# K and V tiles with 32 adjacent keys per partition in a decode attention backward kernel

## The chip, the cores and the metric

The kernel runs on one core of a Trainium2 chip. The metric is the device time of one execution in microseconds; the figure for the kernel before is the median of three runs. A profile of one further execution comes with it: every instruction with its engine, its time and what it waited for, and the packets of the sixteen DMA engines. Engines are PE (TensorE, with PEld for its weight loads), DVE (VectorE), ACT (ScalarE), POOL (GpSimd) and SP (SyncE, which here only issues transfers). HBM is the chip's main memory; SBUF, with 128 partitions, and PSUM, into which PE writes, are the memories on the core.

## The reference

One decode step (four sequences, one new token each, width 512) through a layer norm, an attention over a cache and a gated feed-forward, summed, and then the gradients of all inputs:

```python
def _fwd_reference(A_x, A_k_cache, A_v_cache, A_wq, A_wo, B_x, B_w_gate, B_w_up, B_w_down):
    def _A_ref(x, k_cache, v_cache, wq, wo):
        B, Sq, D = x.shape
        Hq, Dh = 32, 128
        Hkv, Sk = k_cache.shape[1], k_cache.shape[2]
        W = min(4096, max(256, Sk // 4))
        rep = Hq // Hkv
        q = (lambda x, *d: x.transpose(*d))((x @ wq).reshape(B, Sq, Hq, Dh), 0, 2, 1, 3)
        k = jnp.repeat(k_cache[:, :, Sk - W:, :], rep, axis=1)
        v = jnp.repeat(v_cache[:, :, Sk - W:, :], rep, axis=1)
        scores = jnp.einsum("bhqd,bhkd->bhqk", q, k) * (Dh ** -0.5)
        p = _softmax(scores, axis=-1)
        o = jnp.einsum("bhqk,bhkd->bhqd", p, v)
        return (lambda x, *d: x.transpose(*d))(o, 0, 2, 1, 3).reshape(B, Sq, Hq * Dh) @ wo

    def _B_ref(x, w_gate, w_up, w_down):
        return (_gelu(x @ w_gate) * (x @ w_up)) @ w_down

    x = A_x
    xn = _layernorm(x, axis=-1)
    return x + _A_ref(xn, A_k_cache, A_v_cache, A_wq, A_wo) + _B_ref(xn, B_w_gate, B_w_up, B_w_down)
...
    _out, _vjp = jax.vjp(_f, A_x, A_k_cache, A_v_cache, A_wq, A_wo, B_w_gate, B_w_up, B_w_down)
    _grads = _vjp(grad_out)
```

Caches are 4 x 8 x 4096 x 128 in bf16: four sequences (called batches), eight kv heads, 4096 keys of 128 numbers. Only the last W = 1024 keys take part, so the gradients of the two caches are zero in their first 3072 keys and have to be written there all the same. There are 32 query heads, four to a kv head.

## The kernel before

**Stages.** First the feed-forward, forward and backward, with its three weights and their gradients; then attention, batch by batch; then an end with the output, the gradient of x and the gradients of wo and wq. Only the transfers on SP are in an order written out by hand; on the other engines a scheduler orders the instructions by their place in the program and by when it thinks they are ready, and each engine then runs its own list in that order.

**Tiles of K and V.** load_kv brings one batch's K or V (2.1 MB) as a tile of 128 partitions x 8 heads x J = 8 keys x 128 numbers. Key m*8 + j lies in partition m, so each row of a transfer is 8 keys, 2 KB. Two transfers, of four heads each, make a tile (L233). K has two buffers, ka and kb, V one, va. The first K comes by SP's queue, all other tiles by POOL's.

**Attention of one batch.** scores(0, b) makes q times k, scores(1, b) makes dy times v: four VectorE transposes a call (t32, L93), each turning 1024 32-bit words a partition in blocks of 32 x 32 into a scratch tile (two buffers), and 16 matmuls against a block-diagonal tile bd after each; head pair c goes to the partitions of quarter c. softmax makes the probabilities P_b (bf16) and P_f. turned brings P_b's keys onto the partitions by 32 small matmuls and one copy from PSUM through evac. odq multiplies this with V (k = 0, giving the attention output) or K (k = 1, giving the gradient of q), 32 matmuls with the results of head pair c in quarter c; the masks om and oms then pick the right head of a pair. spread makes four scaled copies of P_b, and dvdk from these the gradients of V and K: 64 matmuls, 16 copies out of PSUM into two staging tiles (stg, four buffers for the whole kernel) and two stores of 1 MB on POOL, in rows of 2 KB (L106). softmax_d makes dS_b, which goes through turned, odq and spread in the same way for K.

**Order around the loads.** va for batch b+1 is requested once odq(0, b) has read va; K for batch b+2 once odq(1, b) has read its buffer. zeros puts stores of the zero part on SP's queue (32 in all, 1.5 MB each, rows of 12 KB), no more than three under way, and most of them wait for the landing of the load that is named with them, so that a load goes ahead of them:

```python
                pT = turned(P_b, 0)
                o_done = odq(0, b, pT)
                if b + 1 < B:
                    zeros((2, 2, 4)[b], load_kv(b + 1, 1, att, "va", nc.gpsimd, single_packet=True))
```

**The planner.** evac sends a copy out of PSUM to ScalarE or VectorE, whichever has the smaller sum of charges so far (load["act"], load["dve"]); transposes and other large steps add their own charges.

**bd and dyBD.** bd has two buffers for q (k = 0) and two for dy (k = 1); POOL clears them once at the start of attention and refill writes the blocks. dyBD, 2048 bf16 a partition, is the block-diagonal dy for the products with w_down and wo; it is last read by the do matmuls, before the first batch.

Of the kernel before, what the change touches and what calls it, by code (L numbers as in the profile page):

```python
# [9 lines left out]
ALU = mybir.AluOpType  # L10
# [8 lines left out]
def kernel(  # L19
# [140 lines left out]
    def mask(name, n, in_):  # L160
# [9 lines left out]
    hm = mask("hm", Q, ident_f[:].rearrange("p (h d) -> p h d", d=4))  # L170
    omt = const.tile([P, NQ, 2], FP32, name="omt")
    TT(out=omt[:], in0=gmask[:].rearrange("p (c g) -> p c g", g=2), in1=bm[:].unsqueeze(2).broadcast_to([P, NQ, 2]),
       op=ALU.mult)
    om = mask("om", 2, omt[:].rearrange("p c g -> p g c"))
    oms = const.tile([P, 2], FP32, name="oms")
    TS(out=oms[:], in0=om[:], scalar1=scale, scalar2=None, op0=ALU.mult)
    gmask_b = const.tile([P, G], BF16, name="gmask_b")
# [34 lines left out]
    t32(dyP, pairs(dy_b[:]), 256)  # L212
    dyBD = const.tile([P, NPB, 2, P], BF16, name="dyBD")
    nc.gpsimd.memset(dyBD[:], 0.0)
    dyPb = dyP.bitcast(BF16).rearrange("p n (x r) -> p n r x", r=2)
# [11 lines left out]
    def load_kv(b, k, pool, tag, eng, **kw):  # L227
        d_, src = ((k_t, A_k_cache), (v_t, A_v_cache))[k]
        tl = pool.tile([P, G, J, Dh], BF16, name=tag, tag=tag)
        for hf in range(2):  # L230
            hs = slice(hf * G // 2, (hf + 1) * G // 2)
            with tc.high_priority():
                d = eng.dma_start(out=tl[:, hs].rearrange("p g j d -> p g (j d)"),  # L233
                                  in_=src[b, hs, K0:Sk, :].rearrange("g (m j) d -> m g (j d)", j=J), **kw)
        d_[b] = tl
        return d
# [148 lines left out]
    with tc.tile_pool(name="mid", bufs=1, reuse_waits="tile") as mid:  # L385
# [4 lines left out]
        with tc.tile_pool(name="att", bufs=1, reuse_waits="tile") as att:  # L390
# [7 lines left out]
            for k in range(2):  # L398
                bd.append([])
                for u in range(2):  # L400
                    t_ = att.tile([P, DPB, NQ, 2, 2, Q], BF16, name=f"bd{k}{u}")
                    nc.gpsimd.memset(t_[:], 0.0)
                    bd[k].append(t_)
            selh = att.tile([P, P + 4], FP32, name="selh")
# [61 lines left out]
            def get_d(ps, u):  # L466
                l_ = dsc[:, 512:640] if u == 0 else dsc[:, 640:768]
                mm(ps[:].rearrange("p b d -> p (b d)"), l_, dM.rearrange("p b e k -> p (b e k)"))

            spread_rows(1, get_d)  # L470

# [9 lines left out]
            def scores(k, b):  # L481
# [4 lines left out]
                for g2 in range(2):  # L486
                    for e in range(2):
                        sc = scratch()
                        t32(sc[:].rearrange("p (c j m) -> p c j m", c=NQ, j=J), src[:, g2:G:2, :, e * Q:(e + 1) * Q], 1024)
                        sb = sc[:].bitcast(BF16).rearrange("p (c n r) -> p c r n", c=NQ, r=2)  # L490
                        for r in range(2):
                            for c, q in enumerate(quad):
                                mm(ps[q, :], t_[:, e, c, g2, r, :], sb[:, c, r, :], g2 == 0 and e == 0 and r == 0,
                                   g2 == 1 and e == 1 and r == 1, (0, Q * c))
                return ps[:]

            def spread(src, k):
# [3 lines left out]
                for a in range(4):  # L501
                    TS(out=sp[:, :, a, :], in0=src[:].rearrange("p (j m) -> p j m", j=J), scalar1=amask[:, a:a + 1],  # L502
                       scalar2=None, op0=ALU.mult)
                return sp

            def turned(src, k):

                ps = bank("pT_ps", "x", (P, J, Q))
                for j in range(J):
                    for a, q in enumerate(quad):  # L510
                        mm(ps[q, j, :], src[:, j * Q:(j + 1) * Q], selp[:, a].rearrange("p c r -> p (c r)"), pos=(0, Q * a))
                pT = att.tile([P, J, Q], BF16, name="pT", tag=f"pT{k}")
                evac(pT[:], ps[:], NJ)
                return pT
# [4 lines left out]
            def softmax(S):  # L519
# [18 lines left out]
                nc.vector.reciprocal(out=rr[:], in_=es_ps[:])  # L538
                P_b = att.tile([P, NJ], BF16, name="P_b", tag="P_b")
                nc.scalar.activation(out=P_b[:], in_=E_f[:], func=ACT.Copy, scale=rr[:, 0:1])  # L540
                P_f = att.tile([P, NJ], FP32, name="P_f", tag="P_f")
                p_done = nc.scalar.activation(out=P_f[:], in_=E_f[:], func=ACT.Copy, scale=rr[:, 0:1])
                load["act"] += 1400
                return P_f, P_b, p_done

            def softmax_d(P_f, dP):
# [7 lines left out]
                nc.vector.tensor_copy(out=cc[:], in_=gs_ps[:])  # L554
                dS_b = att.tile([P, NJ], BF16, name="dS_b", tag="dS_b")
                STT(out=dS_b[:], in0=dP, scalar=cc[:, 0:1], in1=P_f[:], op0=ALU.subtract, op1=ALU.mult)
                load["dve"] += 1200
                return dS_b
# [18 lines left out]
            def odq(k, b, pT):  # L577
# [3 lines left out]
                for j in range(J):  # L581
                    for c, q in enumerate(quad):
                        mm(ps[q].rearrange("p g d -> p (g d)"), pT[:, j, :], src[:, 2 * c:2 * c + 2, j, :],
                           j == 0, j == J - 1, (0, Q * c))
                mk = (om, oms)[k]
                t_ = att.tile([P, Dh], FP32, name="odt", tag=f"odt{k}")
# [189 lines left out]
```

## Time and profile before

| what | value |
|---|---|
| median of three runs | 283.15 us (282.53 to 283.21) |
| the profiled execution | 283.66 us, span 281.3 us |
| busy: PE, DVE, ACT, POOL | 184.8, 162.6, 124.3, 60.2 us |
| moved by DMA | 112.21 MB, mean 399 GB/s |
| HBM read, written | 30.93 MB, 81.01 MB |
| DMA issues: zeros; dv, dk, dwo, dwq; va; kb; ka | 32 of 1536 KB; 24 of 1024 KB; 8; 4; 4 of 1024 KB |
| from issue to landing, median: zeros, va, kb | 13.8, 15.8, 20.6 us |

The span runs from the first instruction to the last of the profiled execution. A row of digits divides it into 40 equal slices, each digit the busy share in tenths (9 is 90% or more). q1 is the queue of transfers issued by SP, q0 that of POOL; the last figure of a queue is the time that its packets took, as a share of sixteen engines' span. Matmuls overlap, so that PE's busy time is not a measure of a full PE. In a line of a group, "out<-in" names the tiles, then come partitions x elements, the count, and after the bar the busy time in all (us), the mean of one (ns), and the idle time of the engine before them with what ended it.

### The profile page before, as it was taken

How to read it: one execution, taken by the hardware profiler on the slowest of the kernel's cores; microseconds unless marked ns; L12 is line 12 of the kernel's file. 1: busy time of each engine (PE TensorE's matmuls, PEld its weight loads, DVE VectorE, ACT ScalarE, POOL GpSimd, SP SyncE). 2: the span in 40 equal slices, each digit the busy share in tenths (PEclk: the TensorE clock that was granted, in tenths of full speed). 3: DMA queues.
4: the chain of work that ended last, by engine and by line, in shares of the span. 5: the costliest groups of instructions: out<-in, count | busy, mean ns of one | idle time of the engine just before them, and what ended most of it. 6: DMA issues, size and time to landing. Idle time of an engine off the chain costs nothing.

```text
span 281.3 us, 4405 instructions
## 1 busy us (share of the span) xinstructions
PE 184.8 (66%) x1733; PEld 75.0 (27%) x1733; DVE 162.6 (58%) x309; ACT 124.3 (44%) x245; POOL 60.2 (21%) x135
## 2 busy tenths in 40 slices
PE   0327899869354999559946642953357997944980
PEld 0102363233122624224311321321034232410210
DVE  1869748899796616445028350574396104495980
ACT  1133855720102489525724402722341768544880
POOL 8500110088182213130040060020020020200210
PEclk9999965558855557555555555555555557775555
DMA  7999999999999999999999999999989999999996
GB/s 251 422 445 438 396 392 416 431 425 414 389 430 424 426 364 400 314 379 416 421 406 395 428 429 412 351 430 429 424 354 423 420 404 398 401 412 404 410 384 250
DMA packets 17027, 112.21 MB, mean 399 GB/s; under 512 B 1384, under 2 KB 1648, under 8 KB 11376
## 3 DMA queue, kind: packets, MB, share of 16 engines
q1 hardware_dynamic: 6688, 66.46, 56.9%
q0 software_dynamic: 10176, 45.35, 41.2%
q8 instruction: 13, 0.21, 0.3%
q10 hardware_dynamic: 144, 0.13, 0.1%
q14 instruction: 6, 0.05, 0.1%
HBM read 30.93 MB, written 81.01 MB: 398 GB/s over the span
## 4 chain that ended last, share of the span: by engine, by line
DMA 32%; issue 14%; DVE 10%; PE 9%; ACT 4%; POOL 2%; POOLq 0%; ACTq 0%; DVEq 0%
DMA out_dram<-stg 19%; DMA va<-in_A_v_cache_dram 11%; DVE scr L93 6%; ACT stg L88 3%; PE dwq_ps L117 2%; DMA out_dram<-ztile 2%; PE od_ps L117 2%; PE sc_ps L117 1%; DVE stg L89 1%; POOL out_dram L106 1%; PE kv_ps L117 1%; DVE dqs L603 1%; PE dwo_ps L117 1%; PE es_ps L117 1%; DVE spr L502 1%
## 5 line engine op out<-in xcount | busy, mean ns | idle before, releaser
L88 ACT CAST stg<-kv_ps 128x512 bf16<-128x512 f32 x118 | 63.8, 602 | 57.5 <-DMA out_dram<-stg 29.6
L106 POOL DMA_DIRECT2D out_dram<-stg x30 | 19.7, 659 | 146.2 <-ACT stg L88 105.0
L117 PE MATMUL sc_ps<-scr,bd 128*32 128x256 bf16 x256 | 24.2, 396 | 21.8 <-DVE scr L93 21.8
L117 PE MATMUL kv_ps<-dm,spr 32*128 32x256 bf16 x128 | 28.5, 399 | 6.8 <-ACT stg L88 5.0
L117 PE MATMUL kv_ps<-qm,spr 32*128 32x256 bf16 x128 | 24.5, 371 | 12.1 <-ACT stg L88 11.6
L93 DVE STREAM_TRANSPOSE scr<-va 128x1024 uint32<-128x1024 uint32 x16 | 18.8, 1216 | 12.6 <-DMA va<-in_A_v_cache_dram 12.5
L117 PEld LDWEIGHTS <-spr 32*128 32x128 bf16 x256 | 12.1, 101 | 46.8 <-issue 42.4
L117 PEld LDWEIGHTS <-bd 128*32 128x32 bf16 x256 | 8.1, 107 | 34.7 <-issue 34.1
L88 ACT CAST stg<-dwg_ps 128x448 bf16<-128x448 f32 x26 | 12.5, 554 | 5.8 <-PE dwg_ps L117 3.4
L88 ACT CAST stg<-dwo_ps 128x512 bf16<-128x512 f32 x18 | 10.0, 588 | 11.2 <-PE dwo_ps L117 8.9
L117 PE MATMUL dwo_ps<-dy_b,oSP 32*128 32x512 bf16 x32 | 9.4, 522 | 7.8 <-ACT stg L88 6.6
L89 DVE CAST stg<-kv_ps 128x512 bf16<-128x512 f32 x10 | 6.6, 678 | 12.0 <-DMA out_dram<-stg 6.0
L93 DVE STREAM_TRANSPOSE scr<-ka 128x1024 uint32<-128x1024 uint32 x8 | 9.6, 1228 | 6.1 <-DMA ka<-in_A_k_cache_dram 3.9
L233 POOL DMA_DIRECT2D va<-in_A_v_cache_dram x8 | 6.0, 756 | 31.6 <-PE od_ps L117 27.7
L93 DVE STREAM_TRANSPOSE scr<-kb 128x1024 uint32<-128x1024 uint32 x8 | 9.8, 1231 | 5.1 <-DMA kb<-in_A_k_cache_dram 4.5
L117 PE MATMUL do_ps<-scr,dyBD 128*128 128x512 bf16 x32 | 10.2, 460 | 2.1 <-DVE scr L93 2.0
L117 PE MATMUL dwq_ps<-dqSP,xn_b 32*128 32x512 bf16 x32 | 10.7, 586 | 0.9
L588 DVE SCALAR_TENSOR_TENSOR odt<-od_ps,oms,odt 128x128 f32<-128x128 f32 x4 | 1.4, 340 | 17.2 <-ACT odt L587 17.0
L89 DVE CAST stg<-dwo_ps 128x512 bf16<-128x512 f32 x14 | 9.2, 680 | 3.5 <-issue 2.3
L89 DVE CAST stg<-dwq_ps 128x512 bf16<-128x512 f32 x15 | 9.9, 689 | 1.7 <-PE dwq_ps L117 1.4
L117 PEld LDWEIGHTS <-pT 128*32 128x32 bf16 x256 | 9.2, 140 | 5.2 <-ACT pT L88 2.3
L88 ACT CAST stg<-dwq_ps 128x512 bf16<-128x512 f32 x17 | 9.8, 585 | 1.3 <-PE dwq_ps L117 0.6
(196 smaller groups left out, 317.1 us busy)
## 6 DMA issues: line engine op xcount, KB each, us to landing
out_dram<-ztile SPq DMA_DIRECT2D x32, 1536.0 KB, 13.8
out_dram<-stg POOLq DMA_DIRECT2D x24, 1024.0 KB, 12.8
va<-in_A_v_cache_dram POOLq DMA_DIRECT2D x8, 1024.0 KB, 15.8
out_dram<-stg POOLq DMA_DIRECT2D x6, 896.0 KB, 10.9
wq_sb<-in_A_wq_dram SPq DMA_DIRECT2D x1, 4096.0 KB, 24.1
wo_sb<-in_A_wo_dram SPq DMA_DIRECT2D x1, 4096.0 KB, 34.7
kb<-in_A_k_cache_dram POOLq DMA_DIRECT2D x4, 1024.0 KB, 20.6
ka<-in_A_k_cache_dram SPq DMA_DIRECT2D x2, 1024.0 KB, 43.4
```

What stands on the lines that cost most here:

```text
L88: return nc.scalar.copy(out=out, in_=in_)
L89: return nc.vector.tensor_copy(out=out, in_=in_)
L93: nc.vector.transpose(out=out, in_=in_)
L106: d = eng.dma_start(out=out, in_=in_, **kw)
L117: nc.tensor.matmul(out, lhsT=lhsT, rhs=rhs, start=first, stop=last, **kw)
L233: d = eng.dma_start(out=tl[:, hs].rearrange("p g j d -> p g (j d)"), in_=src[b, hs, K0:Sk, :].rearrange("g (m j) d -> m g (j d)", j=J), **kw)
L502: TS(out=sp[:, :, a, :], in0=src[:].rearrange("p (j m) -> p j m", j=J), scalar1=amask[:, a:a + 1], scalar2=None, op0=ALU.mult)
L588: done = STT(out=t_[:], in0=ps[:, 1, :], scalar=mk[:, 1:2], in1=t_[:], op0=ALU.mult, op1=ALU.add)
L603: nc.vector.tensor_copy(out=dqs[q, :, :, :, a * B + b], in_=d3v[q])
```

## The change

K and V tiles become 128 partitions x 2 heads x 32 keys x 128 numbers: partition 4m + c holds keys 32m to 32m + 31 of the two heads of pair c. A row of a transfer is 32 adjacent keys, 8 KB; a tile takes four transfers of 32 partitions each, one for each c, onto every fourth partition.

What follows from the layout: the transposes in scores write in the order (j, m, c) into a tile that is laid out c, j, m; the scores' columns are then ordered key-in-row j (32) by row m (8 of each quarter). turned makes P transposed four times as large (it needs the probabilities of each key on the partitions of all four c, of which a mask, pmask, keeps one): P_b and dS_b are written four times over (1024 instead of 256 elements), 128 matmuls replace 32, and two masked multiplies on VectorE replace one copy by the planner. odq keeps its count of matmuls; a quarter of the result now holds a quarter of the keys, and the sum over quarters falls to the matmul that follows. spread reads with strides, so that dvdk and its stores keep the old layout of rows. The two bd tiles for dy lie in dyBD's memory, which POOL clears again after the do matmuls. The masks om and oms give way to pmask and g2ms. Charges of the planner: 1400 to VectorE for turned in place of evac's, 2000 for 1400 (ScalarE, softmax) and 2000 for 1200 (VectorE, softmax_d).

```diff
-    omt = const.tile([P, NQ, 2], FP32, name="omt")
-    TT(out=omt[:], in0=gmask[:].rearrange("p (c g) -> p c g", g=2), in1=bm[:].unsqueeze(2).broadcast_to([P, NQ, 2]),
-       op=ALU.mult)
-    om = mask("om", 2, omt[:].rearrange("p c g -> p g c"))
-    oms = const.tile([P, 2], FP32, name="oms")
-    TS(out=oms[:], in0=om[:], scalar1=scale, scalar2=None, op0=ALU.mult)
+    pmask = mask("pmask", NQ, ident_f[:].rearrange("p (m q) -> p q m", q=NQ))
+    g2ms = const.tile([P, 2], FP32, name="g2ms")
+    TS(out=g2ms[:], in0=g2m[:], scalar1=scale, scalar2=None, op0=ALU.mult)
...
-        tl = pool.tile([P, G, J, Dh], BF16, name=tag, tag=tag)
-        for hf in range(2):
-            hs = slice(hf * G // 2, (hf + 1) * G // 2)
+        tl = pool.tile([P, 2, Q, Dh], BF16, name=tag, tag=tag)
+        row = tl[:].ap[0][0]
+        for c in range(NQ):
             with tc.high_priority():
-                d = eng.dma_start(out=tl[:, hs].rearrange("p g j d -> p g (j d)"),
-                                  in_=src[b, hs, K0:Sk, :].rearrange("g (m j) d -> m g (j d)", j=J), **kw)
+                d = eng.dma_start(out=bass.AP(tensor=tl.tensor, offset=tl.offset + c * row,
+                                              ap=[[NQ * row, Q], [Q * Dh, 2], [1, Q * Dh]]),
+                                  in_=src[b, 2 * c:2 * c + 2, K0:Sk, :].rearrange("g (m j) d -> m g (j d)", j=Q), **kw)
...
-                    t_ = att.tile([P, DPB, NQ, 2, 2, Q], BF16, name=f"bd{k}{u}")
-                    nc.gpsimd.memset(t_[:], 0.0)
-                    bd[k].append(t_)
+                    if k == 0:
+                        t_ = att.tile([P, DPB * NQ * 4 * Q], BF16, name=f"bd{u}")[:]
+                        nc.gpsimd.memset(t_, 0.0)
+                    else:
+                        t_ = dyBD_t[:, u * 1024:(u + 1) * 1024]
+                    bd[k].append(t_.rearrange("p (e c g r m) -> p e c g r m", e=DPB, c=NQ, g=2, r=2))
...
+            nc.gpsimd.memset(dyBD_t[:], 0.0)
             spread_rows(1, get_d)
...
-                        t32(sc[:].rearrange("p (c j m) -> p c j m", c=NQ, j=J), src[:, g2:G:2, :, e * Q:(e + 1) * Q], 1024)
+                        t32(sc[:].rearrange("p (c j m) -> p j m c", c=NQ, j=Q), src[:, g2, :, e * Q:(e + 1) * Q], 1024)
...
-                    TS(out=sp[:, :, a, :], in0=src[:].rearrange("p (j m) -> p j m", j=J), scalar1=amask[:, a:a + 1],
+                    TS(out=sp[:, :, a, :].rearrange("p j (m h) -> p j m h", h=4),
+                       in0=src[:, :, 0].rearrange("p (h j m) -> p j m h", h=4, j=J), scalar1=amask[:, a:a + 1],
                        scalar2=None, op0=ALU.mult)
...
-                ps = bank("pT_ps", "x", (P, J, Q))
-                for j in range(J):
-                    for a, q in enumerate(quad):
-                        mm(ps[q, j, :], src[:, j * Q:(j + 1) * Q], selp[:, a].rearrange("p c r -> p (c r)"), pos=(0, Q * a))
-                pT = att.tile([P, J, Q], BF16, name="pT", tag=f"pT{k}")
-                evac(pT[:], ps[:], NJ)
+                pT = att.tile([P, Q, NQ, 8], BF16, name="pT", tag="pT")
+                for h in range(2):
+                    ps = bank("pT_ps", "x", (P, 16, Q))
+                    for j in range(16):
+                        o_ = (16 * h + j) * 8
+                        l_ = src[:, o_:o_ + 8].rearrange("p m c -> p (m c)")
+                        for a, q in enumerate(quad):
+                            mm(ps[q, j, :], l_, selp[:, a].rearrange("p c r -> p (c r)"), pos=(0, Q * a))
+                    load["dve"] += 700
+                    TT(out=pT[:, 16 * h:16 * h + 16], in0=ps[:].rearrange("p j (c r) -> p j c r", c=NQ),
+                       in1=pmask[:].unsqueeze(1).unsqueeze(3).broadcast_to([P, 16, NQ, 8]), op=ALU.mult)
...
-                P_b = att.tile([P, NJ], BF16, name="P_b", tag="P_b")
-                nc.scalar.activation(out=P_b[:], in_=E_f[:], func=ACT.Copy, scale=rr[:, 0:1])
+                P_b = att.tile([P, NJ, NQ], BF16, name="P_b", tag="P_b")
+                nc.scalar.activation(out=P_b[:], in_=E_f[:].unsqueeze(2).broadcast_to([P, NJ, NQ]), func=ACT.Copy,
+                                     scale=rr[:, 0:1])
...
-                dS_b = att.tile([P, NJ], BF16, name="dS_b", tag="dS_b")
-                STT(out=dS_b[:], in0=dP, scalar=cc[:, 0:1], in1=P_f[:], op0=ALU.subtract, op1=ALU.mult)
+                dS_b = att.tile([P, NJ, NQ], BF16, name="dS_b", tag="dS_b")
+                STT(out=dS_b[:], in0=dP.unsqueeze(2).broadcast_to([P, NJ, NQ]), scalar=cc[:, 0:1],
+                    in1=P_f[:].unsqueeze(2).broadcast_to([P, NJ, NQ]), op0=ALU.subtract, op1=ALU.mult)
...
-                    for c, q in enumerate(quad):
-                        mm(ps[q].rearrange("p g d -> p (g d)"), pT[:, j, :], src[:, 2 * c:2 * c + 2, j, :],
-                           j == 0, j == J - 1, (0, Q * c))
-                mk = (om, oms)[k]
+                    for a, q in enumerate(quad):
+                        mm(ps[q].rearrange("p g d -> p (g d)"), pT[:, 4 * j + a].rearrange("p c r -> p (c r)"),
+                           src[:, :, 4 * j + a, :], j == 0, j == J - 1, (0, Q * a))
+                mk = (g2m, g2ms)[k]
```

## The prediction

> **What bounds the kernel now.** I read the slices of the page first, then its DMA queues, then stretches of the span side by side, then the chain of waits, and last the groups of single instructions. The first two, from the page:
>
> ```profile
> DMA  7999999999999999999999999999989999999996
> q1 hardware_dynamic: 6688, 66.46, 56.9%
> q0 software_dynamic: 10176, 45.35, 41.2%
> ```
>
> The two queues' packets fill 98.1% of sixteen engines' span, and no slice but the ends falls below 0.8. The kernel is bound by its transfers: every microsecond in which they stop is lost, and every byte that moves faster is won. How fast bytes move in each kind of stretch (columns: busy time of each engine, clock, DMA share, GB/s):
>
> ```profile
> core 0: us, PE busy (x) PEld busy (x) DVE busy (x) ACT busy (x) POOL busy (x), PEclk, DMA share, GB/s
> 70.00:77.00 7.00, 2.75 (x17) 0.86 (x15) 5.37 (x13) 1.18 (x2) 0.68 (x4) 0.88 1.02 388
> 80.00:94.00 14.00, 8.08 (x134) 4.69 (x137) 11.46 (x20) 1.85 (x5) 6.21 (x28) 0.50 1.00 425
> 98.00:105.00 7.00, 6.87 (x67) 1.95 (x67) 1.23 (x5) 5.71 (x11) 0.92 (x4) 0.50 0.91 359
> 112.00:122.00 10.00, 6.42 (x93) 3.27 (x92) 4.63 (x13) 5.04 (x12) 0.76 (x1) 0.54 0.96 310
> 259.00:273.00 14.00, 12.47 (x39) 2.89 (x39) 12.26 (x19) 12.28 (x23) 2.67 (x5) 0.50 0.98 403
> ```
>
> From 70 to 77 only K and V arrive, in 2 KB rows; from 80 to 94 mostly zeros leave, in 12 KB rows; from 259 to 273 only 8 KB rows leave. VectorE is the reader's second look: 11.46 of 14 us busy from 80 to 94, so in that stretch the program beside the transfers is VectorE's. Where the two meet, in the chain of waits (start, length, work):
>
> ```profile
> 91.73 0.59 PE sc_ps L117 x5
> 92.31 1.75 PE od_ps L117 x25
> 94.06 0.29 issue
> 94.34 9.05 DMA va<-in_A_v_cache_dram
> 103.41 5.83 DMA out_dram<-ztile
> ```
>
> The second V tile is asked for when od of batch 0 has read the first, and the zeros behind it wait for its landing. What the queues moved from 98 to 105:
>
> ```profile
> q0 software_dynamic: 532, 2.06, 75.5%
> q1 hardware_dynamic: 50, 0.43, 14.6%
> ```
>
> Of the five zero stores allowed before this load (7.9 MB, 18.5 us at 425 GB/s from about 79.5) almost nothing is left at 98. So V had 98.3 - 94.3 = 4 us of cover, and beyond it od of batch 0 sets when transfers go on.
>
> **The gain: rows of 8 KB.** Busy engines moved 388/1.02 = 380 GB/s in 2 KB rows and 403/0.98 = 411 in 8 KB rows, the latter in stores. A tile of 2.1 MB takes 5.52 us by the one, 5.10 by the other: 0.42 us, 3.3 us for eight tiles. Bounds: nothing, if row length isn't what costs reads; 6 us, if also the stretch 112 to 122 (3.1 MB in 10 us, 7.5 us at 411) recovers. I take 3.3. The tiles ka(0), va(0) and kb(1) land ahead of the gap described below and only open it earlier, so five tiles count: **-2.1 us**.
>
> **The price: transposes that write scattered words.** scores has the same 32 transposes of 1024 words, but each now writes neighbouring elements 1 KB apart (order j, m, c with c outermost in the tile), where before runs of 32 stood together. The trace has no such transpose. The nearest groups:
>
> ```profile
> L93 DVE STREAM_TRANSPOSE scr<-kb 128x1024 uint32<-128x1024 uint32 x8 | 9.8, 1231 | 5.1 <-DMA kb<-in_A_k_cache_dram 4.5 <-PE sc_ps L117 0.6
> L603 DVE COPY dqs<-d 32x128 bf16<-32x128 bf16 x16 | 7.0, 435 | 0.3
> L702 DVE COPY dn<-dn_ps 4x128 f32<-4x128 f32 x4 | 1.1, 378 | 1.2 <-PE dn_ps L117 1.2
> L93 DVE STREAM_TRANSPOSE aT<-a_b 128x448 bf16<-128x448 bf16 x1 | 1.0, 971 | 0.0
> L382 DVE COPY dxf<-dxf_ps 128x128 f32<-128x128 f32 x1 | 0.3, 272 | 0.0
> ```
>
> dn writes 128 words 16 bytes apart, dxf 128 words side by side: 106 ns more, 0.83 ns an element, 0.85 us for 1024. aT reads 28 bytes apart: against 632 ns (between the transposes of 256 at 445 and of 512 at 694) it pays 339 ns, 0.76 each, 0.78 us for 1024. dqs writes 32 bytes apart: at least (435 - 272)/128 = 1.27, 1.3 us. Lower end nothing, as no row is itself a scattered transpose; the d4mask scaling (L463), which reads 128 bytes apart, shows 339 ns for 128 elements against 278 for 256 together, an unclear case. I take dn, a write of 4-byte words: **1.23 becomes 2.08 us**. By the Trainium skill ("Advanced Engine Details and Errata", SBUF Cachelines) SBUF has 16-byte lines, needs two hits on each to hide its latency, and a new line for each access is penalised; dn and aT agree, and by that rule alone the term is above nothing, without a figure.
>
> **The same chain's smaller terms.** P_b grows from 256 to 1024 outputs: by 508 ns for 256 and 693 for 512 (qm, L432), +0.55 us. turned issues 128 matmuls, not 32; 32 took 0.41 us (90.69 to 91.10), so halves of 0.82 us, each followed by a VectorE multiply out of PSUM of 512 elements (0.69, s_o L674): 2.3 us against 0.41 + 0.37, **+1.5**. spread's four scalings read with strides: 0.28 to between 0.28 and 0.68, I take 0.45; 1.8 us now stand on VectorE ahead of the first multiply, which is ready after 0.82: **+1.0** (0 to 2). dS_b, 464 ns, grows to about 1.2 us at the transposes' 0.97 ns an element, and its turned as P_b's, but both are off the V chain.
>
> **The gap.** Eleven transposes stand before od of batch 0: 11 x 0.85 = 9.35, with the rest 12.4 us. V is asked for at 106.7 and flows from 107.7; the zeros end at 98: **+9.7 us** with idle transfers. From there transfers have again 16.3 MB (two loads, dv, dk, five zeros; 40 us) against a VectorE-ScalarE chain that grows from 28 to some 35 us, and in the next batches 16.3 us from landing to od grows by about 9 beside 38 us of transfers; cover holds, priced 0 to 6, I take 0. In the last batch VectorE does four more such transposes and the wider steps (3.4 + 0.55 + 0.7 + 1.5 = 6 us) between the staging release at 201 and the dv store at 228, where about 3 us of queued zeros are left: 3 us, less what is won because the second pT no longer waits in ScalarE's row of casts (229.8): 0 to 3, **+1.5**.
>
> **At nothing.** The masks (om, oms out; pmask, g2ms in) run while VectorE waits 4.7 us for dy_b. dyBD is cleared again on POOL (1.8 us) after the do matmuls, ahead of refill, for two bd clears of 0.97 dropped; refill of D3d waits 6.9 us there anyway, uncovered 1.8. Four load issues of 64 rows for two of 512: POOL spent 0.75 on 512 rows and 0.53 on 128, so at most 2.1 for 1.5; behind them wait dv's stores, which queue on full engines; else 0.6 a tile. On SP the two more issues precede a zero that waits until 35. The od matmuls keep number and shape. The planner's charges, followed through the loops, give ScalarE 127 of 128 kv casts for 118, 5.4 us, beside 18.8 busy of 40 a batch.
>
> **Sum**, on the profiled execution's 283.66 (span 281.3 and 2.4 around it): +9.7 - 2.1 + 1.5 = 292.8; that run lies 0.5 above the median, so **292.3 us**.
>
> **Rivals.** *A, loads win:* scattered writes cost nothing. Then od is late by 3.1 us, inside the 4 of cover; -3.3 and +1 in the last batch: 280.9. For it, L463; against it, dn, dqs, aT. The point from which it decides is about 0.1 us a transpose. *B, VectorE becomes the bound:* 1.3 us a transpose gives 5 us more in the gap and 1.8 at the end, and each of three batches loses its margin by about 1: 302. dqs speaks for it, 17.9 busy of 40 us against it. *C, cancels:* about 0.3 us a transpose, 6.4 us of delay less 4 of cover, less the loads: 283. *D, 32 partitions starve the engines:* loads at half the 388 GB/s cost 5.4 us more each; with zeros beside half of them, about +25 over the sum, 317. Against it, the zeros leave from 64 partitions, every second one, at 425. By the Trainium skill ("DMA: Bandwidth & Descriptors", Rules for kernel authors) full rate wants 128 partitions and 1 MiB a transfer, and this change has 32 and half; by the fixed 2 us a transfer of its Anatomy of one DMA, four for two would, as an estimate, add 4 us a tile where nothing lies beside; the four load transfers that POOL issued from 57.4 to 59.7 ran one behind the other at full engines, which doesn't show it.
>
> **Numbers.** Forecast 0.50 (287 to 299), A 0.23, B 0.16, C 0.06, D 0.05. Under 0.3% (0.85 us) this kernel's runs tell nothing. Faster is A, same is C, slower the rest: 0.23, 0.06, 0.71. The range 280.3 to 305 leaves out the lower third of A (more than 3.3 won), D and the tail of B.
>
> **What would show it.** Right: transposes of va, ka, kb near 2.1 us; POOL's second V load at about 107; a slice near 100 to 107 with low DMA share; read stretches above 400 GB/s. Wrong: transposes at 1.23 with that load before 99 (A); at 2.5 and VectorE full in every batch (B); read stretches near 200 (D).

## The result and the profile after

The changed kernel takes **317.12 us** (median; 316.32 to 318.09) against 283.18 for the kernel before: ratio 1.1188, 95% interval 1.1149 to 1.1227, some 34 us slower. Forecast was 292.3, range 280.3 to 305. The profiled execution took 318.09 us with a span of 316.1, against 281.3 before.

The slices and queues of the page of after:

```profile
DMA  7999999999993043999699999999558999999794
GB/s 274 431 453 431 365 424 428 422 425 425 432 434 144 19 185 117 369 420 426 249 344 424 429 430 360 423 433 417 210 209 334 418 423 384 419 398 401 321 376 188
q1 hardware_dynamic: 5952, 66.46, 50.3%
q0 software_dynamic: 8608, 45.35, 36.6%
```

The queues' packets fill 86.9% of the span, 98.1% before. Transfers did not become slower; they stop, in four places. The same view of stretches as before (busy time of each engine, clock, DMA share, GB/s):

```profile
core 0: us, PE busy (x) PEld busy (x) DVE busy (x) ACT busy (x) POOL busy (x), PEclk, DMA share, GB/s
70.00:77.00 7.00, 2.35 (x9) 0.67 (x7) 6.05 (x10) 0.00 (x0) 6.71 (x9) 0.93 1.02 426
97.00:109.00 12.00, 6.35 (x192) 3.78 (x192) 8.15 (x14) 3.43 (x7) 0.96 (x5) 0.50 0.06 22
113.00:123.00 10.00, 9.72 (x196) 3.79 (x195) 4.48 (x9) 5.51 (x11) 0.25 (x1) 0.50 0.16 58
150.00:157.00 7.00, 2.83 (x35) 1.68 (x36) 2.59 (x6) 0.63 (x2) 2.72 (x6) 0.50 0.61 231
224.00:238.00 14.00, 12.37 (x75) 3.21 (x73) 4.69 (x4) 11.80 (x24) 2.59 (x4) 0.50 0.44 164
```

Where only loads ran (70 to 77), transfers onto 32 partitions in 8 KB rows moved 426 GB/s; before, 388. Idle transfers, as length times what is missing of the share: 11.3 us at 97 to 109 (the gap that was forecast), then 8.4, 2.7 and 7.8, which were not: 30 of the 35 us of span. The groups that the forecast had priced:

```profile
L93 DVE STREAM_TRANSPOSE scr<-va 128x1024 uint32<-128x1024 uint32 x16 | 29.5, 1945 | 4.0 <-PE sc_ps L117 4.0
L521 DVE TENSOR_TENSOR pT<-pT_ps,pmask 128x512 bf16<-128x512 f32 x16 | 10.8, 697 | 15.5 <-PE pT_ps L117 15.5
L505 DVE TENSOR_SCALAR spr<-P_b,amask 128x256 bf16<-128x256 bf16 x16 | 6.4, 470 | 2.6 <-ACT P_b L549 2.6
L549 ACT ACTIVATE P_b<-E_f,rr 128x1024 bf16<-128x1024 f32 x4 | 4.6, 1148 | 3.8 <-DVE rr L547 3.8
```

The scattered transposes take 1.945 us (1.23 before; 2.08 forecast). Two views show what stops the transfers. POOL's instructions from 106 to 126:

```profile
108.96 1.59 POOL L231 DMA_DIRECT2D va<-in_A_v_cache_dram  x3 [6.43 <-PE od_ps L117]
122.75 0.54 POOL L231 DMA_DIRECT2D ka<-in_A_k_cache_dram  x1 [12.20 <-PE od_ps L117]
123.28 0.53 POOL L231 DMA_DIRECT2D va<-in_A_v_cache_dram  x1
123.81 1.60 POOL L231 DMA_DIRECT2D ka<-in_A_k_cache_dram  x3
```

V's fourth transfer stands behind one of the next K, which waits 12.2 us for od; zeros and scores wait for the whole of V. The stores of dv, first issued at 105.06 before, stand behind these loads too and begin at 157. And ScalarE ahead of the softmax of batch 3, with SP's wait for it below:

```profile
201.59 5.97 ACT L88 CAST stg<-kv_ps 128x512 bf16<-128x512 f32 x12
211.06 1.07 ACT L88 CAST stg<-kv_ps 128x512 bf16<-128x512 f32 x2 [3.49 <-DMA out_dram<-stg]
220.38 6.95 ACT L88 CAST stg<-kv_ps 128x512 bf16<-128x512 f32 x14 [8.24 <-DMA out_dram<-stg]
...
236.92 0.56 ACT L543 ACTIVATE E_f<-sc_ps,negm 128x256 f32<-128x256 f32 x1
```
```profile
SPq L106 <- ACT P_f L552: 27.0, 1, 27.0
```

Forty-three casts of dv and dk stand between od(1,2) (k = 1, batch 2) and this exponential; before there were eight, and it came at 203.80. That the casts hold it is seen on VectorE, which had the other thing that it waits for, negm, ready 14 us earlier:

```profile
222.82 0.16 DVE L540 COPY negm<-nm_ps 128x1 f32<-128x1 f32 x1 [6.72 <-PE nm_ps L117]
```

Three zero stores are released by P_f, behind the exponential, and wait 27 us. In the kernel before SP has no wait for P_f.

### The profile page after: what moved, and what is told of

The parts are those of the page before. It is cut to its first block, busy times and chain, and to the rows that moved or that the text cites. A ratio compares the mean times of both kernels' runs of the same rounds, so it can differ in the third digit from the quotient of the medians.

```text
span 316.1 us, 5981 instructions
## 1 busy us (share of the span) xinstructions
PE 203.6 (64%) x2501; PEld 83.6 (26%) x2501; DVE 197.5 (62%) x312; ACT 129.8 (41%) x249; POOL 65.0 (21%) x148
## 4 chain that ended last, share of the span: by engine, by line
PE 38%; DVE 21%; DMA 12%; ACT 12%; issue 12%; POOL 1%; SPq 1%; POOLq 0%; DVEq 0%; ACTq 0%
DVE scr L93 12%; PE kv_ps L117 9%; DMA out_dram<-stg 9%; ACT stg L88 9%; DMA wu_sb<-in_B_w_up_dram 3%; PE dwg_ps L117 3%; PE od_ps L117 3%; PE sc_ps L117 2%; PE dwq_ps L117 2%; PE ok_ps L117 2%; PE do_ps L117 2%; PE ob_ps L117 2%; PE pT_ps L117 2%; PE dwo_ps L117 1%; PE dxq_ps L117 1%
## 5 line engine op out<-in xcount | busy, mean ns | idle before, releaser
L93 DVE STREAM_TRANSPOSE scr<-va 128x1024 uint32<-128x1024 uint32 x16 | 29.5, 1945 | 4.0 <-PE sc_ps L117 4.0
L117 PE MATMUL kv_ps<-qm,spr 32*128 32x256 bf16 x128 | 30.8, 397 | 1.3 <-ACT stg L88 1.1
L117 PE MATMUL sc_ps<-scr,bd 128*32 128x256 bf16 x128 | 11.5, 402 | 15.6 <-DVE scr L93 15.3
L521 DVE TENSOR_TENSOR pT<-pT_ps,pmask 128x512 bf16<-128x512 f32 x16 | 10.8, 697 | 15.5 <-PE pT_ps L117 15.5
L117 PE MATMUL sc_ps<-scr,dyBD 128*32 128x256 bf16 x128 | 12.0, 401 | 11.2 <-DVE scr L93 11.2
L117 PEld LDWEIGHTS <-dyBD 128*32 128x32 bf16 (+1 forms) x176 | 9.7, 110 | 31.9 <-issue 28.5
L93 DVE STREAM_TRANSPOSE scr<-kb 128x1024 uint32<-128x1024 uint32 x8 | 15.4, 1944 | 0.4 <-PE sc_ps L117 0.4
L117 PE MATMUL od_ps<-va,pT 128*32 128x256 bf16 x128 | 9.7, 414 | 7.6 <-DVE pT L521 4.5
L93 DVE STREAM_TRANSPOSE scr<-ka 128x1024 uint32<-128x1024 uint32 x8 | 14.5, 1920 | 0.0
L88 ACT CAST stg<-dwo_ps 128x512 bf16<-128x512 f32 x21 | 11.3, 602 | 7.1 <-PE dwo_ps L117 7.0
L117 PE MATMUL pT_ps<-selp,dS_b 128*32 128x32 bf16 x512 | 8.9, 194 | 4.6 <-issue 2.3
L117 PE MATMUL do_ps<-scr,dyBD 128*128 128x512 bf16 x32 | 10.1, 454 | 2.2 <-DVE scr L93 2.1
```

Of the source, the lines that this page charges most:

```text
L88: return nc.scalar.copy(out=out, in_=in_)
L93: nc.vector.transpose(out=out, in_=in_)
L117: nc.tensor.matmul(out, lhsT=lhsT, rhs=rhs, start=first, stop=last, **kw)
L521: TT(out=pT[:, 16 * h:16 * h + 16], in0=ps[:].rearrange("p j (c r) -> p j c r", c=NQ), in1=pmask[:].unsqueeze(1).unsqueeze(3).broadcast_to ...
```

## The experiments

Four causes were possible: the scatter (S), the wide steps (W: fourfold P_b and dS_b, 128 small matmuls, masked multiplies, strided spread), the four load transfers by themselves (L), and the order that the scheduler gave the engines' lists. All figures are ratios to the kernel before on the same chip; microseconds are the ratio less one, times 283.2.

**First round: the order on POOL, and the scatter.** The run e1_order adds edges that fix the order of issue and nothing else:

```diff
+        prior = {0: (last.get("load"), first.get((0, b - 2))), 1: (last.get("load"), first.get((1, b - 2)))}[k]
...
+            for o in prior:
+                if o is not None and eng is nc.gpsimd:
+                    issued_after(d.ins, o.ins)
```

> The changed kernel with nothing but POOL's list put back into the order of the kernel before: the four transfers of a tile in one piece, and the dv and dk stores ahead of the next loads, by scheduling edges without a semaphore. Theory 1 (the order of POOL's list is most of the loss: the fourth V transfer and then the first three stores stood behind K loads that waited for od): the idle transfers at 113 to 123, 151 to 157 and 224 to 238 us go, 25 us, while the gap at 98 to 109 stays: 290 to 297 us. Theory 2 (the scattered transposes are all of it): 312 to 318. Theory 3 (the wider steps on PE, ScalarE and VectorE are it): over 305.

Measured 313.54 us, 1.1079 (1.1044 to 1.1113). A miss for the first theory: 3 us less than the changed kernel, not 20 or more. Its list was also one store off: K(3) and V(3) stood behind a store that stood behind them before. The exact list comes below.

The run e2_contiguous lets the transposes write side by side and PE read with strides instead; e3_both adds e1's order to it:

```diff
-t32(sc[:].rearrange("p (c j m) -> p j m c", c=NQ, j=Q), ...
-sb = sc[:].bitcast(BF16).rearrange("p (c n r) -> p c r n", c=NQ, r=2)
+t32(sc[:].rearrange("p (j m) -> p j m", j=Q), ...
+sb = sc[:].bitcast(BF16).rearrange("p (n c r) -> p c r n", c=NQ, r=2)
```

> The changed kernel with the 32 transposes writing blocks of 32 words together, and the matmuls of the scores reading every fourth word pair instead; POOL's list as in the changed kernel. All theories: transposes back from 1.94 to about 1.23 us, the matmuls of the scores at about 0.40 us unless strided reading costs PE. Theory 1: the gap at 98 to 109 shrinks by some 8 us and the later idle stretches stay, 306 to 311 us. Theory 2: below 292. Theory 3: 312 to 318.

> Both edits together: POOL's list in the old order and transposes that write together. Theory 1 with the transposes as the rest: 280 to 287 us, and below 283 if the loads in rows of 8 KB win 3 us. Theory 2: as the run with contiguous transposes alone. Theory 3: over 295, with the chain of waits in the 128 small matmuls, the fourfold P_b and the masked multiplies.

Measured 313.52 (1.1082, 1.1055 to 1.1109) and 304.5 (1.0764, 1.0741 to 1.0787). The repair has a price of its own; two groups of e2_contiguous:

```profile
L117 PE MATMUL sc_ps<-scr,dyBD 128*32 128x256 bf16 x128 | 20.8, 625 | 2.0 <-DVE scr L93 1.9
L93 DVE STREAM_TRANSPOSE scr<-va 128x1024 uint32<-128x1024 uint32 x16 | 19.3, 1228 | 6.0 <-PE sc_ps L117 5.6
```

The transposes are back at 1.23 us, but each matmul of the scores, which now reads numbers 16 bytes apart instead of 4, takes 0.625 us, 0.401 in the changed kernel. With the transposes so, e1's edges return 9.0 us (e3 against e2), three times what they return in e1. Both runs fall where the third theory, the wide steps, had put them; e8 below prices those steps alone. The run e4_before_scatter is the kernel before with only the scattered writes, and measures the scatter cleanly:

```diff
-t32(sc[:].rearrange("p (c j m) -> p c j m", c=NQ, j=J), src[:, g2:G:2, :, ...
+t32(sc[:].rearrange("p (c j m) -> p j m c", c=NQ, j=Q), src[:, 4*g2:4*g2+4, :, ...
```

> The kernel before with only the transposes' writes scattered 1 KB apart, as in the changed kernel; the scores' columns then come in another order, so the outputs are not the reference's, but every instruction keeps its size. It prices the scattered writes by themselves. Theory 1: transposes at 1.94 us, eleven of them before od of batch 0, 8 us less 4 us of cover, and 3 in the last batch: 287 to 292 us. Theory 2: over 305. Theory 3: 283 to 286.

Measured 289.88, 1.025 (1.0205 to 1.0295), transposes 1.93 us: S costs **7.1 us** alone.

**Second round: each part alone.** e5_loads_alone puts the new load_kv of the change's diff into the kernel before; e7_loads_ordered adds e1's edges; e8_wide_alone takes the changed kernel and puts loads and transposes back. e6_rows_8k keeps two transfers of 128 partitions and makes each row 8 KB:

```diff
-in_=src[b, hs, K0:Sk, :].rearrange("g (m j) d -> m g (j d)", j=J)
+in_=src[b, hf].rearrange("(m j) d -> m (j d)", j=Q)
```

> The kernel before with the new loads alone: four transfers a tile, each 32 partitions (every fourth) by two heads by 8 KB, into a tile that everything else reads as before; transposes, P_b, turned, spread and od are those of before. The data then lie in other places than the reading assumes, so dk, dv, dx, dwq and dwo come from mixed-up keys; work and bytes are those of before. The scheduler's list on POOL is split as in the changed kernel: three of V's four transfers, then K's, V's fourth after a K transfer that waits for od. Theory 'the split list on POOL': the fourth V transfer waits for another tile's od, the stores wait behind it, transfers stop two or three times, 290 to 298 us. Theory 'wide steps': the split list costs little when the chain of VectorE and ScalarE is as short as before, and the faster rows give something back: 280 to 286.

> The kernel before with its two transfers a tile kept at 128 partitions, but each partition gets one row of 8 KB (32 adjacent keys of one head) instead of four rows of 2 KB; the heads read are the first two only, over all 4096 keys, so all that follows from K and V is computed from other data. Everything else, the list on POOL too, is that of before. Row length by itself: if 8 KB reads flow at the 425 to 431 GB/s that the changed kernel showed where only loads ran, against 388 before, five loads that count win 2 to 3 us, 280 to 281.5. If the transfers that overlap them set the total, 282.5 to 283.5.

> As the run with the new loads alone (outputs from mixed-up keys, same work and bytes), with edges that only fix the order of POOL's list: a tile's four transfers stand together, each behind the first store that stood ahead of it before. All theories that put the remaining loss on the wide steps (fourfold P_b and dS_b, 128 small matmuls, masked multiplies) expect no loss here: 280 to 283.5. If four transfers of 32 partitions cost by themselves (issue time on POOL, engines starved), above 286.

> The changed kernel with the loads and the transposes of before put back (two transfers a tile, runs of 32 words together), so that only the wide steps stay: P_b and dS_b written four times over, 128 instead of 32 small matmuls to turn each, the masked multiplies out of PSUM on VectorE, one pT buffer for two, the scalings of spread read with strides, the smaller masks. Their columns no longer match the keys, so dq's and o's share of the outputs is computed from mixed-up keys. Theory 'wide steps': the 21 us that stay when order and scatter are undone are these, 295 to 303 us. My recorded sum gave them +0.55, +1.5 and +1.0 on the V chain and 1.5 at the end: 284 to 288 if it holds. If they are hidden: 283.

Measured: e5 295.14, 1.0406 (1.0348 to 1.0463), 11.5 us; e6 283.4, 0.999 (0.9961 to 1.002), nothing that differs from zero (-1.1 to +0.6 us); e7 287.55, 1.0129 (1.0067 to 1.0191), 3.7 us; e8 288.18, 1.0161 (1.0114 to 1.0207), 4.6 us. So the split list is dear in the loads alone (7.8 us between e5 and e7), and longer rows win nothing. The 4.6 us of the wide steps are near the recorded terms, 3.05 in the chain and 1.5 at the end, but that is luck: the recorded sum also had 4 us of cover, behind which 3.05 us alone would cost nothing, and 1.5 was for scatter and wide steps together. In e8 transfers are idle for 4.3 us from 97 to 109 (share 0.64). Why longer rows win nothing, by the stretches of e6_rows_8k (the first fence) and of the kernel before (the second; 98 to 105 was 0.91 there):

```profile
core 0: us, PE busy (x) PEld busy (x) DVE busy (x) ACT busy (x) POOL busy (x), PEclk, DMA share, GB/s
98.00:105.00 7.00, 6.90 (x68) 2.96 (x68) 2.17 (x8) 4.35 (x9) 0.92 (x4) 0.50 0.98 390
262.00:281.00 19.00, 9.45 (x29) 2.00 (x26) 9.59 (x15) 8.95 (x16) 2.45 (x5) 0.50 0.78 318
```
```profile
262.00:281.00 19.00, 10.78 (x33) 2.35 (x31) 10.70 (x17) 10.28 (x19) 2.66 (x5) 0.50 0.85 348
```

Bytes are ahead until 262; then transfers wait for the casts of dwo and dwq, 0.78 busy instead of 0.85, which gives 1.3 us back.

**Third round: do they add?** e10_scatter_wide is W with e4's edit; e11_loads_scatter is e7 with it; e12_loads_wide is e1 with the transposes of before; e9_clears_first is e7 with one edge more, K(1)'s load behind POOL's clears.

> As the run with ordered loads (outputs from mixed-up keys, same work and bytes), but K's second load is issued behind POOL's clearing of bd, selh and dqs. In the runs with four load transfers a tile POOL's fourth transfer of that K waited 5.1 us and the store behind it 3.3 us, each for the landing of an earlier transfer that uses the same of eight semaphores; the clears fell to 70.7 to 76.3 and VectorE's two casts of hm beside them took 3.65 us instead of 0.18, so that everything up to the second V load came 4.3 us later. Theory 'POOL held by its own transfers': with the clears ahead the casts take 0.2 us again, V is asked for at 94 to 95, and the 3.9 us of that run go: 282.5 to 284.5. Rival 'four transfers of 32 partitions cost by themselves': 286 to 289.

> The loads of before, with scattered transposes and the wide steps (columns no longer match the keys: o's and dq's share of the outputs is computed from mixed-up keys). Alone they cost 6.8 and 4.5 us. Theory 'they add': 293.5 to 295.5. Theory 'the margin of each batch is spent': past some length the chain from V's landing to the next V load outlasts the transfers of a batch, and every further microsecond costs three or four: 298 to 305.

> The kernel before with the new loads in fixed order and scattered transposes, without the wide steps (outputs from mixed-up keys). Alone they cost 3.9 and 6.8 us. If they add: 293 to 295. If a batch's margin is spent already by these two: 298 or more.

> The changed kernel with POOL's list in order and the transposes of before (runs of 32 words together), so new loads and wide steps without the scatter (outputs from mixed-up keys). It is the run with order and scatter undone but without PE's reading of every fourth word pair, which took 0.63 instead of 0.40 us a matmul there (304.5). If loads and wide steps add: 291 to 293, and the other 12 us of that run are PE's strided reading. If wide steps and loads spend the margin together: 300 to 305.

| parts | run | us | ratio (95%) | over before | sum of the parts alone |
|---|---|---|---|---|---|
| S + W | e10 | 297.17 | 1.0436 (1.0355 to 1.0517) | 12.4 | 11.7 |
| L + S | e11 | 298.22 | 1.0490 (1.0421 to 1.0560) | 13.9 | 10.8 |
| L + W | e12 | 300.17 | 1.0553 (1.0488 to 1.0618) | 15.7 | 8.3 |
| L + S + W | e1 | 313.54 | 1.1079 (1.1044 to 1.1113) | 30.6 | 15.4 |

Scatter and wide steps add (e10 lies between its two expected ranges, and its interval, 10.1 to 14.6 us, holds the sum). With the new loads, each costs more than alone; what makes it so is only in part found below. e9 (287.85, 1.012, 1.0054 to 1.0187) missed: its casts of hm were back at 0.18 us and V was asked for at 96.51 instead of 98.62, but the time stayed that of e7.

**Fourth round: POOL's list exact, and its clears.** f1_exact_order, f2_loads_exact and f3_loads_wide_exact mend e1's edges; f5_exact_clears is f1 with e9's edge.

```diff
+    after = {(2, 0): [(0, 0, 0)], (2, 1): [(1, 0, 0)], (3, 0): [(1, 0, 1)], (3, 1): [(0, 1, 1)]}
```

Each load, named by batch and k, stands behind a store, named by k (0 for dv, 1 for dk), batch and half.

> The changed kernel, all of it, with POOL's list now store for store as before. In the earlier run with a fixed list the edges had put K(3) behind dv's first store of batch 1 and V(3) behind dk's, where before those loads stood ahead of them; in the traces that store waits some 20 us for ScalarE's casts while transfers stop. Theory 'the list': scatter and wide steps added to 12.4 alone, loads cost 3 to 4; with the list right the three add, 297 to 301, and the rest of the 34 us is the list. Rival 'four small transfers lengthen each batch': 308 to 313, as with the first edges.

> The kernel before with the new loads alone, POOL's list store for store as before (outputs from mixed-up keys, same work and bytes). With the list one store off it was 3.7 us slower. Theory 'the list': 283 to 285.5. Rival 'four small transfers': 286.5 to 289 again.

> New loads and wide steps without the scatter (outputs from mixed-up keys), POOL's list store for store as before. With the list one store off 15.7 us, against 8.3 for the two alone. Theory 'the list': 288 to 293. Rival 'loads and wide steps spend the margin together': 298 to 301.

> The changed kernel, all of it, with POOL's list as before but for K's load of batch 1, which is issued behind POOL's clearing of bd, selh and dqs. In the changed kernel these clears ran from 70.8 to 76.5 beside VectorE, whose four scalings by d4mask took 2.65 us instead of 1.07. If the hold on POOL counts, V is asked for some 2 to 3 us earlier than in the run with the exact list and the time is 2 to 3 us less; if the early stretch is hidden or paid back by K's later landing, within 1 us of it.

Measured: f1 315.98, 1.1158 (1.1122 to 1.1195); f2 289.88, 1.0197 (1.0127 to 1.0267); f3 300.43, 1.0602 (1.0541 to 1.0663); f5 313.3, 1.106 (1.1021 to 1.1099). For the whole change the theory of POOL's list falls: f1 lies above both its ranges, and the exact list returns 0.8 us, less than the intervals tell apart. In f1 the stretches that it was to mend are full, and the time is lost later:

```profile
113.00:123.00 10.00, 9.36 (x184) 3.69 (x184) 4.64 (x9) 5.34 (x10) 0.77 (x1) 0.50 1.01 407
150.00:157.00 7.00, 3.48 (x162) 2.66 (x163) 4.41 (x10) 1.28 (x4) 1.99 (x4) 0.69 0.97 349
210.00:237.00 27.00, 18.30 (x115) 5.11 (x115) 18.13 (x15) 14.78 (x29) 3.01 (x4) 0.50 0.45 177
```

27 x 0.55 = 14.9 us of idle transfers now lie before the softmax of batch 3. In S + W on the loads of before (e10) the same stretch is full:

```profile
210.00:235.00 25.00, 17.05 (x304) 8.81 (x305) 18.50 (x27) 9.15 (x18) 0.86 (x2) 0.50 1.01 423
```

f5 hit: 2.8 us less than f1, and V asked for at 106.7 instead of 109.6. What it was to mend, in POOL's waits and VectorE's instructions of the changed kernel:

```profile
POOL kb L231 <- DMA out_dram<-stg: 5.1, 1, 5.1
POOL out_dram L106 <- DMA va<-in_A_v_cache_dram: 2.4, 1, 2.4
```
```profile
73.68 0.92 DVE L461 CAST scr<-hm 128x128 bf16<-128x128 f32 x1
74.59 2.65 DVE L465 TENSOR_SCALAR scr<-scr,d4mask 128x128 bf16<-128x128 f32 x4
```

In these traces an issue on POOL waits for the landing of the transfer eight issues before it: K's fourth for a store that stands eight ahead, the store behind it for V's first. (That it comes of eight semaphores used in turn, as the text on e9 has it, the traces do not show; they show the count.) Four transfers a tile come round sooner: K's fourth waited 5.1 us, the store behind it 2.4, and the clears of bd and dqs fell to 70.76 to 74.51, beside VectorE's casts (0.92 instead of 0.18) and ahead of dyBD's clear, beside which the scalings ran (2.65 for four instead of 1.07). The same in f5:

```profile
73.08 0.90 DVE L476 CAST scr<-hm 128x128 bf16<-128x128 f32 x1
73.97 1.21 DVE L480 TENSOR_SCALAR scr<-scr,d4mask 128x128 bf16<-128x128 f32 x4
```

Only the scalings recover. The casts still end with a clear, now that of dyBD (72.10 to 73.90); e8 and e10 show the same 0.90 on the old loads. So the second clear of dyBD, a part of the wide steps, costs the chain some 0.9 us by itself.

**Fifth round: the lists of ScalarE and VectorE.** Casts of dv and dk in ScalarE's list between the steps of batches 1 to 3, counted in the traces:

| kernel | before od(0,1) | before od(1,1) | before softmax 2 | before od(0,2) | before od(1,2) | before softmax 3 | exp of softmax 3 at |
|---|---|---|---|---|---|---|---|
| before | 0 | 18 | 11 | 0 | 15 | 8 | 203.8 |
| S + W (e10) | 3 | 13 | 16 | 3 | 13 | 15 | 209.7 |
| after | 0 | 0 | 0 | 2 | 18 | 43 | 236.9 |
| f1 | 1 | 3 | 16 | 12 | 0 | 31 | 237.2 |
| g3 | 0 | 16 | 16 | 0 | 16 | 15 | 228.0 |

With the new loads ScalarE waits for od with casts standing behind it, and does them ahead of the last softmax instead. g3_engine_lists mends this on f5 with edges: the last of K's transposes, and for batches 1 and 2 also the second of V's, ahead of the last step of od(1) of the batch before on VectorE, and thirteen casts of dv ahead of od(1)'s copy on ScalarE. (The text below names K's and the casts; the edit has V's too, and K's from batch 1 on.) g2_lists_spoiled makes the reverse of K's edges on e10:

```diff
+                        if k == 0 and b > 0 and (g2, e) == ahead:                 # g3, K's transposes
+                            issued_after(od_done[1, b - 1].ins, d.ins)
+                        if k == 1 and 0 < b < B - 1 and (g2, e) == (0, 1):        # g3, V's
+                            issued_after(od_done[1, b - 1].ins, d.ins)
...
+                if k == 1 and 0 < b < B - 1:                                      # g3, the casts
+                    issued_after(d.ins, casts[0, b][12].ins)
...
+                        if k == 0 and b > 1:                                      # g2
+                            issued_after(d.ins, turned_row[b - 1].ins)
```

> The run of the whole change with exact store order and early clears (313.3), with two more kinds of edges that fix only the order of engines' lists, nothing of the work: on VectorE the transposes of the next K tile stand ahead of od(1,b)'s last step for batches 1 and 2, on ScalarE 13 of dv's casts stand ahead of od(1,b)'s copy. Without them ScalarE's list has 0 to 4 casts before that copy and 31 before the softmax of batch 3, where the run with scatter and wide steps on the old loads (297.2) has 13 and 15, and the kernel before 11 to 18 and 8. Theory 'the scheduler's lists on VectorE and ScalarE': the exponential of batch 3 comes at 215 to 225 instead of 234, the 15 us of idle transfers from 210 to 235 shrink to 5 or less, 299 to 305. Rival 'four small transfers lengthen each batch': 311 to 315.

> The run with scatter and wide steps on the loads of before (297.2; o's and dq's share of the outputs from mixed-up keys), spoiled by one kind of edge: the transposes of K for batches 2 and 3 stand behind od(1) of the batch before on VectorE, as in the changed kernel's list; no load, byte or instruction changes. Theory 'the lists': ScalarE's exponential of batch 3 comes some 8 to 15 us later than its 210.0, transfers idle there, 303 to 312. Rival: 296 to 299, the place of K's transposes alone costs nothing, and it takes the late casts or the new loads.

g3: 305.58, 1.0773 (1.0745 to 1.0802), 8.1 us less than f5 with the same instructions. The exponential came at 228.0, less early than expected, and what was idle from 210 to 235 shrank from 15 (share 0.40 in f5) to 6.8 us:

```profile
210.00:235.00 25.00, 18.17 (x239) 6.65 (x238) 15.54 (x26) 13.74 (x28) 3.01 (x4) 0.50 0.73 284
```

g2: 297.3, 1.0489 (1.0465 to 1.0514) against e10's 297.17, 1.0436 (1.0355 to 1.0517): there the place of K's transposes costs nothing that can be told: its exponential comes at 214.90 instead of 209.67, but the transfers stay full (1.01 from 210 to 235). That does not tell which of g3's edges returns the 8.1 us where transfers had stopped; they were not tried apart. The traces of f5 and g3 (in this order) speak against the casts on ScalarE alone, because ScalarE stands idle ahead of the exponential and VectorE releases it:

```profile
233.56 0.47 ACT L558 ACTIVATE E_f<-sc_ps,negm 128x256 f32<-128x256 f32 x1 [2.08 <-DVE negm L555]
228.03 0.48 ACT L565 ACTIVATE E_f<-sc_ps,negm 128x256 f32<-128x256 f32 x1 [2.13 <-DVE negm L562]
```

K's transposes of batch 3 begin at 208.81 in f5 and at 201.46 in g3, 7.4 us earlier, and the exponential comes 5.5 us earlier; between them PE does matmuls of dv and dk. On VectorE g3 still turns wq (194.7 to 201.5) ahead of K's transposes. Why four transfers a tile lead the scheduler to these lists was not tested either.

## Why the prediction was right and wrong

Where the 33.7 us are, by one path through the runs: 12.4 for scatter and wide steps on the old loads; 8.1 for the lists of ScalarE and VectorE; 2.8 for POOL's held clears (in the loads alone, e9 against e7, they cost nothing); 0.8 between the scheduler's list on POOL and the exact one (after against f1, intervals that overlap). Of the 9.5 that remain in g3 beyond S + W, fixed loads alone account for 3.4 to 5.6 (e9, e7, f2), and 4 to 6 us stay open: g3 has 6.8 us of idle transfers from 210 to 235, where e10 has none, and why, no run shows.

- **Scatter and wide steps: right, the sum in part by luck.** Transposes 1.945 for 2.08 us, P_b 1.15 for 1.06, the masked multiply 0.697 for 0.69, spread 0.47 for 0.45. The two parts, +9.7 and +1.5, stand against 12.4 measured (e10). Counted from the start of the hm casts to V's request, the chain grew by 7.0 us for the scatter (e4; forecast 9.35), 3.7 for the wide steps (e8; 3.05) and 11.2 for both (e10; 12.4), so errors of both signs met. Of the 3.7, some 0.9 is the second clear of dyBD, which the prediction had under "At nothing".
- **The gap: right in place and near in size.** V asked for at 108.96 (forecast 107), 11.3 us idle (9.7). Counted as above, the chain grew by 13.6 us: the 11.2 of e10, and 2.4 more with POOL's held clears, which were not seen. The remaining 1.0 us is that the chain began later in this execution (casts at 73.68, 72.64 before).
- **Rows of 8 KB, -2.1: the rate right, the term mis-sized.** 426 GB/s where loads run alone, more than the 411 assumed; but the run with longer rows alone measures 0 (e6). The kernel's end is set by casts there, and what is won early is waited for late. The sum took a faster transfer for a shorter kernel without asking what bounds the last 20 us.
- **"From there ... cover holds, priced 0 to 6, I take 0": the step that failed.** The changed kernel lost 18.9 us there. The reasoning compared lengths of chains with 40 us of transfers, and on the old loads it nearly held: e10 has full transfers from 150 to 157 and from 210 to 235, and loses 1.8 us from 113 to 123, with the same VectorE work. What it took for given was that each engine keeps its order. It did not: V's fourth transfer went behind the next K, which stops the transfers from 113 to 123 and near 150, and 43 casts ahead of the last softmax, which stops them from 224 to 238. The traces show these waits; edges that change order alone return 8.1 us (g3) and 2.8 us (f5) of the loss, while POOL's order by itself returns next to nothing, because the transfers then stop later (f1).
- **"At nothing: four load issues": failed with it.** Their time on POOL was right (0.54 us each), and the time was not what mattered. Loads alone cost 11.5 us with the scheduler's list and 3.4 to 5.6 with a fixed one; that only dv's stores stand behind them was wrong.
- **The planner's charges: right.** ScalarE took 127 of 128 casts.
- **Last batch, +1.5:** not separable in the runs.
- **Rivals.** A fell with the transposes, C with it. B came nearer in time (302) but by 1.3 us more a transpose, where the trace shows 0.7, and with VectorE full in every batch, where it is 62% busy. D's 317 is the measured time, but by luck: it needed loads at half rate, near 200 GB/s, and they ran at 426. The Trainium skill ("DMA: Bandwidth & Descriptors", Rules for kernel authors) wants 128 partitions and 1 MiB a transfer for full rate; here 32 partitions and 512 KB moved more than 128 and 1 MiB, in 2 KB rows (388) and in 8 KB rows (419, e6), so the measurement decides against it. What the Trainium skill states of new lines ("Advanced Engine Details and Errata", SBUF Cachelines) agrees with the trace in direction, 1.23 to 1.945 us.

No run beat the kernel before; e6 can't be told from it.

## What to carry to other kernels

When an edit changes the number or the waits of transfers, ask what order the scheduler will give every engine's list, not only what each instruction costs: list the steps in order on each engine, before and after, ahead of comparing durations. Edges that change the order and nothing else can return several microseconds (8.1 here). And price a faster transfer by what bounds the end of the kernel: bytes that arrive early are worth nothing where casts set the pace.

## What the runs showed of the hardware

- A VectorE transpose of 1024 words that writes 1 KB apart takes 1.92 to 1.945 us instead of 1.23: 0.70 ns a word.
- A matmul of the scores (128 x 256 out) that reads bf16 numbers 16 bytes apart takes 0.625 us (e2); 4 bytes apart, 0.401.
- Loads of 8 KB rows ran at 419 (128 partitions, e6) and 426 GB/s (32, every fourth), 2 KB rows at 388.
- VectorE's casts of hm waited for POOL's clears: 0.92 us, ending at 74.60 when POOL's clear of dqs ended at 74.51. The Trainium skill ("SBUF — State Buffer", SBUF: two separate sides) calls the port pair that the two share an exclusive lock, held for the whole instruction; the trace agrees.
